# Attention with compressive memory and a gMLP mixer: the order of small work in each attention step, and the end of the attention phase

## The chip, the cores and the metric

The kernel runs on one core of a Trainium2 chip. The metric is the time of one execution on the device in microseconds, as a median over several runs. A core has engines that each run their own list of instructions in order: PE (matrix products, into PSUM), DVE (vector work), ACT (functions and casts), POOL (more vector work), and SP, which here issues nearly all DMA transfers. They wait for one another through semaphores.

## The reference

x has 2048 rows of 640. Two equal layers follow one another; each adds an attention block and then a mixer block to x, and each block begins with a layer norm:

```
x = x + A(layernorm(x));  x = x + B(layernorm(x));  x = x + A(layernorm(x));  x = x + B(layernorm(x))

A: q, k, v = x @ wq, x @ wk, x @ wv          # 32 heads of 20, 4 segments of 512 rows
   for each segment:
       p     = softmax(q k^T / sqrt(20) + mask)   # mask: 0 where the key is at or before the query, else -1e9
       a_dot = p @ v
       a_mem = (phi(q) @ M) / (phi(q) @ z + 1e-6) # phi(t) = t + 1 if t > 0, else exp(t)
       o     = g * a_mem + (1 - g) * a_dot        # g = sigmoid(beta), one per head
       M, z  = M + phi(k)^T @ v, z + sum of phi(k)
   return o @ wo

B: z = gelu(x @ w_in);  z1, z2 = halves of z
   g = w_sp @ layernorm(z2) + b_sp                # w_sp mixes the 2048 rows
   return (z1 * g) @ w_out
```

All is float32. Products are formed from fp16 pairs: each operand is split into a high part and a low part (the cast, and what the cast left), and high times high, high times low and low times high are summed in PSUM.

## The kernel before

Each layer has three stages. **phase1a** is the attention, **phase1b** the layer norm and the first product of the mixer (w_in) with its gelu, **phase2** the mixing over rows and the product with w_out. The change touches phase1a and the seam to phase1b.

*phase1a* (the class Attention) handles 64 pairs of heads, 16 in each of the 4 segments. `run` walks over steps t from -16 to 164, five for every two pairs. Each step writes instructions for different pairs at different distances: `by_queries` forms scores mp whose row maxima mxs are taken on DVE (L1316, L1319); `by_keys` forms scores es transposed, whose exponential P (named Pb for some pairs) is taken on ACT (L1293); `cast` makes P's high part PH on ACT (L1328) and its low part PL (L1332), in two halves of 640 columns, on POOL; `pvs` multiplies PH and PL with the values into one PSUM bank named pv (L1366); `combine` scales that by the row sums and adds it to the memory's part, on DVE (L1377 to L1387, the last addition into gm at L1387). The bank pv has one buffer: pv of a pair starts when combine of the pair before has read its bank out.

Between these stand denser pieces of work, interleaved by their planned times: `unit` makes the queries and keys of 128 channels (five units to a segment, unit (0,0) the first; L1111, tiles qps and kps), with the splits and features of `out` behind them (L1125 to L1156: khl, qhl, relu, phl); `value` the values (vps, L1052); `project` the output product for 12 of the 16 row tiles (yps, L1084); `update` adds a unit's keys and values to the memory (mup, L1209) and copies the result, masked, to mst (L1215); `read` multiplies mst with the query features (num, L1180); `prep` takes the row norms of the next row tiles of x (statistics L305 to L308, the norm at L1033, splits L320 and L321, a DMA transpose L322) into xt. The last pair of a unit also writes out the unit's output halves ohl (casts L1402 and L1403, DMA L1406). num, mup and some small products share a second bank, tagged "ms", with one buffer.

PE's order is the order in which all this is written. What DVE, ACT, POOL and SP do, and in what order, a scheduler sets from the order of writing, from priorities and from named instructions that must be issued first (`issue_after`). Small work that must not stand in front of others is put off with `post(k, f)` to a list `later` of the step k on, and from there it is written before that step's products; a second list, `half`, is written in the middle of the step.

The last pairs have no later work beside them. With TAIL = 1, the low parts of pair 63 are made by POOL for its first head, and for its second head by DVE, written two steps later.

*phase1b* goes over 16 row tiles in the order 0, 8, 1, 9, and so on. For each, `attn_out` takes the rows x1 (loaded at L359; for tiles 12 to 15 it first makes their output product yp, L378), their statistics and norm (for tiles 0 and 8 xn on ACT at L391 and xnhl at L400 and L401), and the split is transposed by DMA into th (L402). Then two products with halves of w_in give zp (L412) for z1 and z2, followed by gelu (L425, L448). In layer 1 the first half of w_in comes as raw chunks wst (L129), split into wi (L81, L82). x1 has two buffers, xn and xnhl one each.

Of the kernel before, what the change touches and what calls it, by code (L numbers as in the profile page):

```python
# [8 lines left out]
F32 = mybir.dt.float32  # L9
# [328 lines left out]
def phase1b(g, o_d, x, x1_d, z1_d, zh, zl):  # L338

    nc, tc = g.nc, g.tc  # L340
    with ExitStack() as ctx:
# [4 lines left out]
        if not g.wsp_scaled:  # L346
            nc.sync.dma_start(g.bsp, g.b_sp.rearrange("(t p) -> p t", p=128))
        g.wi[0].paired(wp0)
        wi0 = g.wi[0].load(g.prep[0], 864, "wr")
# [66 lines left out]
        z2 = {}  # L416
        g.loaded, g.gelu, g.lo = {}, {}, {}

# [31 lines left out]

        with tc.high_priority(offset=3 * HP2):
            a = load(0)
        with tc.high_priority(offset=HP2):
            xn = attn_out(0, *a)
            a = load(ORDER[1])
            th = xn_t(*xn)
        for i, t in enumerate(ORDER):
# [3 lines left out]
            if i + 1 < NT:  # L461
                xn = attn_out(ORDER[i + 1], *a)
            z2_half(t, w_in_half(1, *th))
# [454 lines left out]
class Attention:  # L918
# [9 lines left out]
    def __init__(self, g, x, o_d, x1_d):  # L928
        self.g, self.nc, self.tc = g, g.nc, g.tc
        self.x, self.o_d, self.x1_d = x, o_d, x1_d  # L930
        self.st = g.st
        self.gm = {}
        self.phq = {}
        self.P = {}
        self.pv, self.sum, self.o = {}, {}, {}
        self.mem, self.last, self.stacked, self.waiting = False, -1, -1, False
        self.now, self.later, self.half, self.rd = None, {}, {}, set()
        self.lead = []

    def post(self, k, f, c=None, into=None):  # L940

# [4 lines left out]
        while c is not None and (t % 5 not in c or t in self.rd or t - 1 in self.rd):  # L946
            t += 1
        (self.later if into is None else into).setdefault(t, []).append(f)

# [147 lines left out]
    def unit(self, s, m):  # L1097

        g, nc = self.g, self.nc
        xh, xl = self.xt[s % 2][:, 0], self.xt[s % 2][:, 1]  # L1100
        for nm in "qk" if s else "kq":
            if nm == "k" and self.mem:
# [95 lines left out]
    def update(self, s, m):  # L1198
# [19 lines left out]

        self.post(1, out)

    def stack(self, nm, s, m, hl):
# [5 lines left out]
        nc.sync.dma_start(rows[:, i:i + 2], hl)  # L1227
        if nm == ("k" if s else "q"):
            self.stacked = NU * s + m
# [92 lines left out]
    def cast(self, n, h):  # L1322
# [6 lines left out]

        def low(engine):  # L1330
            for c in (slice(0, 640), slice(640, 1280))[::-1 if n % 2 and h else 1]:
                engine.tensor_tensor(PL[:, c], P[:, h, c], PH[:, c], ALU.subtract)  # L1332

        if h == 0 or n < self.N - self.TAIL:
            low(nc.gpsimd)
        else:
            self.post(2, lambda: low(nc.vector))
        self.P[n, h] = (PH, PL)
# [14 lines left out]
    def pvs(self, n, h, s, m, h0):  # L1353
        nc = self.nc
        PH, PL = self.P.pop((n, h))
        if h == 0:
            pv = self.po.tile([128, 512], F32, tag="pv", name="pv")
            self.pv[n] = pv[:, :8 * 42].rearrange("p (h t c) -> p t h c", h=2, t=4)
            self.sum[n] = pv[:, 8 * 42:8 * 62].rearrange("p (h t c) -> p h t c", h=2, t=4)
# [10 lines left out]
    def combine(self, n, s, m, h0):  # L1370
# [5 lines left out]
        rs = self.pl2.tile([128, 4, 2], F32, tag="rs", name="rs")  # L1376
        nc.vector.tensor_tensor(rs, T[:, :, :, DH], g.iomg[:, h0:h0 + 2].unsqueeze(1).to_broadcast((128, 4, 2)), ALU.mult)  # L1377
        nc.vector.reciprocal(rs, rs)
# [3 lines left out]
        if s > 1:  # L1382
# [3 lines left out]
            nc.vector.tensor_tensor(a, a, wide(DH), ALU.mult)  # L1386
            nc.vector.tensor_tensor(o, a, o, ALU.add)  # L1387
        else:
# [18 lines left out]

        self.post(2, out)

    def run(self, nseg=NSEG):  # L1410
# [82 lines left out]
        def fills():  # L1493

            for t, k, i in sorted(ev):
# [3 lines left out]
                else:  # L1499
                    for d, f in zip((2, 4), self.prep(i)):  # L1500
                        self.post(d, f)

# [57 lines left out]
        for t in range(-LEAD, END):  # L1560
# [33 lines left out]
            with self.behind(DVE):  # L1594
                until(t + 1)
        assert not self.half
        for t in sorted(self.later):
            self.now = None
            for f in self.later[t]:
                f()  # L1600

# [74 lines left out]
```

## Time and profile before

| | |
|---|---|
| median of 3 runs | 2218.08 us (2214.55 to 2218.99) |
| profiled execution | 2217.2 us, its span 2215.5 us |
| mean granted clock of PE | 0.991 |
| PE busy | 2087.8 us, 94% of the span |
| DVE, POOL, ACT busy | 1625.6, 1402.7, 1250.9 us |
| attention of layer 1 | from 0 to about 594 us |
| mixing over rows in layer 1 | 840 to 1115 us |
| attention of layer 2 | from about 1115 to 1677 us |

A row of the timeline has the start, the duration, the engine, the source line, the operation, its result and operands, and in brackets how long the engine stood idle before it and what it waited for. With xN, N neighbouring instructions are one row and the duration is that of all. A row of the waits has the waiting instruction, what released it, the time in all, the number of waits, and the longest. A row of windows has a stretch of time, its length, the busy time of PE, PEld, DVE, ACT and POOL, then PE's granted clock, the DMA share and GB/s.

### The profile page before, as it was taken

The page shows a single profiled execution, that of the slowest core. Times are in us where ns is not written, and L with a number is a line of the kernel's source. Part 1 is how long each engine was busy: PE and PEld are TensorE (multiplying, and loading weights), DVE is VectorE, ACT ScalarE, POOL GpSimd, SP SyncE. Part 2 cuts the span into 40 slices and gives each one's busy share as a digit, 9 for nine tenths or more (in the row PEclk, how much of TensorE's full clock was granted, in tenths as well). Part 3 has the DMA queues.
Part 4 walks back from the last instruction along what each step waited for, and adds up shares of the span by engine and source line. Part 5 has one row for each costly group of instructions (what it writes and reads, how often), then busy time and mean ns, then how long its engine had stood idle before and what let it go on. Part 6 is the DMA issues. An engine that isn't in the chain of part 4 may idle for free.

```text
span 2215.5 us, 53079 instructions
## 1 busy us (share of the span) xinstructions
PE 2087.8 (94%) x21322; PEld 1265.2 (57%) x21322; DVE 1625.6 (73%) x2889; ACT 1250.9 (56%) x1641; POOL 1402.7 (63%) x1172
## 2 busy tenths in 40 slices
PE   5998888999899999999999989989999999999999
PEld 3555655666545555555555556656665555555555
DVE  7788788788587758888657787787875764675563
ACT  4588788788644433333326987878884433333331
POOL 3387898788645345566414889888894433674660
PEclk9999999999999999999999999999999999999999
DMA  6666557344776686666455456553455335876752
GB/s 177 163 174 184 133 163 197 96 121 126 185 199 182 162 278 171 170 183 178 137 167 131 112 139 153 126 118 90 123 141 145 106 110 185 217 175 171 177 142 82
DMA packets 537703, 342.79 MB, mean 155 GB/s; under 512 B 411600, under 2 KB 463312, under 8 KB 537456
## 3 DMA queue, kind: packets, MB, share of 16 engines
q1 hardware_dynamic: 537456, 339.39, 57.2%
q8 instruction: 167, 2.74, 0.5%
q14 instruction: 80, 0.66, 0.1%
HBM read 159.18 MB, written 92.55 MB: 114 GB/s over the span
## 4 chain that ended last, share of the span: by engine, by line
PE 67%; DVE 14%; ACT 7%; issue 4%; DMA 4%; POOL 3%; SPq 1%; ACTq 0%; DVEq 0%; POOLq 0%
PE ga L670 12%; PE zp L412 11%; PE cyp L706 7%; PE pv L1366 4%; PE qps L1111 4%; PE vps L1052 3%; PE gb L670 3%; PE mp L1255 3%; PE yps L1084 3%; DVE mxs L1319 3%; PE gc L670 3%; PE gd L670 3%; PE kps L1111 2%; PE es L1255 2%; ACT PH L1328 2%
## 5 line engine op out<-in xcount | busy, mean ns | idle before, releaser
L1332 POOL TENSOR_TENSOR PL<-P,PH 128x640 f16<-128x640 f32 x384 | 535.1, 1422 | 86.7 <-PE pv L1366 67.9
L1319 DVE TENSOR_REDUCE mxs<-mp 128x2 f32<-128x1024 f32 (+2 forms) x384 | 320.2, 861 | 123.4 <-PE mp L1246 121.3
L1293 ACT ACTIVATE P<-es,sc 128x1024 f32<-128x1024 f32 (+1 forms) x256 | 271.6, 1061 | 102.0 <-PE es L1246 95.8
L640 POOL TENSOR_TENSOR ts<-ts,wt 128x512 f32<-128x512 f32 x196 | 283.3, 1457 | 11.0
L412 PEld LDWEIGHTS <-th 128*128 128x128 f16 x1920 | 188.0, 98 | 169.6 <-issue 6.9
L1328 ACT CAST PH<-P 128x1280 f16<-128x1280 f32 x192 | 239.7, 1249 | 2.5 <-PE pv L1366 1.0
L670 PEld LDWEIGHTS <-wts 128*128 128x128 f16 x1536 | 150.2, 98 | 134.0 <-issue 5.5
L670 PE MATMUL ga<-zh,wts 128*128 128x432 f16 x768 | 210.8, 346 | 4.5 <-ACT u L737 4.5
L308 POOL TENSOR_TENSOR lnrs<-lnve,mhalf 128x1 f32<-128x1 f32 x96 | 59.8, 631 | 230.2 <-DVE lnve L307 223.1
L1332 POOL TENSOR_TENSOR PL<-Pb,PH 128x640 f16<-128x640 f32 x124 | 175.8, 1447 | 20.3 <-PE pv L1366 19.3
L412 PE MATMUL zp<-wi,th 128*128 128x432 f16 x960 | 181.2, 346 | 3.5 <-ACT z L448 3.5
L640 POOL TENSOR_TENSOR ts<-wt,wt 128x512 f32<-128x512 f16 x28 | 33.9, 1211 | 226.3 <-DMA wt<-wn 226.3
L1052 PE MATMUL vps<-wvh,xt 128*128 128x320 f16 x640 | 154.8, 309 | 23.7 <-DVE relu L1143 13.0
L670 PEld LDWEIGHTS <-wt 128*128 128x128 f16 x1152 | 112.7, 98 | 96.5
L1366 PE MATMUL pv<-vs,PH 128*128 128x41 f16 x2560 | 158.6, 182 | 8.6 <-DVE gm L1387 5.5
L706 PE MATMUL cyp<-wuh,ut 128*128 128x320 f16 (+1 forms) x896 | 163.6, 299 | 2.7 <-DMA ut<-un 1.8
L706 PEld LDWEIGHTS <-ut 128*128 128x128 f16 (+1 forms) x1344 | 131.1, 98 | 57.5 <-DMA ut<-un 4.0
L1255 PEld LDWEIGHTS <-qk 64*128 64x128 f16 (+1 forms) x2048 | 77.9, 94 | 150.1 <-issue 129.3
L1366 PE MATMUL pv<-vs,PL 128*128 128x41 f16 x2560 | 156.3, 181 | 2.6 <-POOL PL L1332 2.6
L412 PE MATMUL zp<-wi1h,th 128*128 128x432 f16 x640 | 149.9, 349 | 2.2 <-DMA th<-xnhl 2.1
L524 DVE SCALAR_TENSOR_TENSOR wn<-wr,wsc,wn 128x512 f16<-128x512 f32 x126 | 92.9, 775 | 76.8 <-ACT wn L523 76.7
L1366 PEld LDWEIGHTS <-PH 128*128 128x128 f16 x2560 | 138.6, 96 | 15.2 <-ACT xnhl L400 2.9
(224 smaller groups left out, 5286.5 us busy)
## 6 DMA issues: line engine op xcount, KB each, us to landing
qk<-st SPq DMA_DIRECT2D x256, 120.0 KB
wr<-in_B_w_sp_dram SPq DMA_DIRECT2D x60, 512.0 KB
z<-z SPq DMA_DIRECT2D x32, 432.0 KB
cz<-z SPq DMA_DIRECT2D x32, 432.0 KB
xt<-in_A_x_dram SPq DMA_DIRECT2D x32, 320.0 KB
st<-khl SPq DMA_DIRECT2D x40, 256.0 KB
st<-qhl SPq DMA_DIRECT2D x40, 256.0 KB
x<-x SPq DMA_DIRECT2D x32, 320.0 KB
```

Source lines behind the costliest of these rows:

```text
L412: nc.tensor.matmul(zp[:, n, :FHH], a[:, k, :], b[:, k, c:c + FHH], start=(k == 0 and j == 0), stop=(k == KD - 1 and j == 2))
L640: nc.gpsimd.tensor_tensor(t, a, t if b == "t" else get(b), ALU.add if op == "+" else ALU.subtract)
L670: nc.tensor.matmul(ps, w[:, a, k % 4, :], z[:, k, j, :], start=start and k == 0 and i == 0, stop=k == NP - 1 and i == 2, skip_group_check= ...
L706: nc.tensor.matmul(yp[:, n, :320], a[:kn[k], k, :], b[:kn[k], k, n * 320:(n + 1) * 320], start=(k == 0 and j == 0), stop=(k == KO - 1 and ...
L1052: nc.tensor.matmul(ps, a[:, k, c], b[:, k, n * 320:(n + 1) * 320], start=(i == 0), stop=(i == 14))
L1111: nc.tensor.matmul(ps, a[:, k, c], b[:, k, :], start=(i == 0), stop=(i == 14))
L1255: nc.tensor.matmul(out[:, h, o:o + w], a[r, ac], b[r, bc], start=o == 0, stop=False, skip_group_check=True)
L1293: g.exp = nc.scalar.activation(P, E, AF.Exp, scale=g.esc)
L1319: e = nc.vector.tensor_reduce(mx[:, :, n, j], mp[:, :, o:o + w], AX.X, ALU.max)
L1328: nc.scalar.copy(PH, P[:, h])
L1332: engine.tensor_tensor(PL[:, c], P[:, h, c], PH[:, c], ALU.subtract)
L1366: nc.tensor.matmul(pv[:, i, h, :41], x[:, c:c + 128], v[:, j, h0 + h, :], start=(j == 0 and x is PH), stop=(j == i and x is PL), skip_grou ...
```

## The change

Five edits, all of order or place; what is computed stays the same.

1. phase1b issues the loads of its first two row tiles (0 and 8) first of all, at a high priority, ahead of the chunks of w_in. Tile 0's norm is issued after the last addition of combine(60) (`g.near[-4]`), tile 8's after that of combine(61).
2. A third list, `end`, is written last in each step. `prep`'s row norms and the output halves of `combine` go there. `update`'s memory copy goes first into its step's list (`first=True`).
3. Unit (0,0) makes its queries first, then its keys, as all units of later segments do.
4. The low parts of pair 63 are made for both heads at once, the first half by POOL, the second by DVE.
5. pv of pairs 61 and 63 takes the bank "ms" instead of the bank pv. The first instruction of combine(62) is issued after the last low part.

```diff
+        g.loaded, g.gelu, g.lo = {}, {}, {}
+        two = [pe2.tile([128, D], F32, tag="x1", name="x1") for _ in range(2)]
+        with tc.high_priority(offset=HP):
+            for t, x1 in zip(ORDER, two):
+                g.loaded[t] = nc.sync.dma_start(x1, x1_d[t])
         g.wi[0].paired(wp0)
...
-        with tc.high_priority(offset=3 * HP2):
-            a = load(0)
         with tc.high_priority(offset=HP2):
-            xn = attn_out(0, *a)
-            a = load(ORDER[1])
+            with tc.issue_after(g.near[-4].ins):
+                xn = attn_out(0, two[0])
+            a = two[1:]
             th = xn_t(*xn)
...
             if i + 1 < NT:
-                xn = attn_out(ORDER[i + 1], *a)
+                with ExitStack() if i else tc.issue_after(g.near[-3].ins):
+                    xn = attn_out(ORDER[i + 1], *a)
...
-    def post(self, k, f, c=None, into=None):
+    def post(self, k, f, c=None, into=None, first=False):
...
-        (self.later if into is None else into).setdefault(t, []).append(f)
+        todo = (self.later if into is None else into).setdefault(t, [])
+        todo.insert(0 if first else len(todo), f)
...
-        for nm in "qk" if s else "kq":
+        for nm in "qk" if s or m == 0 else "kq":
...
-        self.post(1, out)
+        self.post(1, out, first=True)
...
-        def low(engine):
-            for c in (slice(0, 640), slice(640, 1280))[::-1 if n % 2 and h else 1]:
-                engine.tensor_tensor(PL[:, c], P[:, h, c], PH[:, c], ALU.subtract)
-
-        if h == 0 or n < self.N - self.TAIL:
-            low(nc.gpsimd)
-        else:
-            self.post(2, lambda: low(nc.vector))
+        for i, c in enumerate((slice(0, 640), slice(640, 1280))[::-1 if n % 2 and h else 1]):
+            self.low = (nc.vector if i and n >= self.N - self.TAIL else nc.gpsimd).tensor_tensor(PL[:, c], P[:, h, c], PH[:, c], ALU.subtract)
...
-            pv = self.po.tile([128, 512], F32, tag="pv", name="pv")
+            p, tag = (self.pm, "ms") if n in (self.N - 3, self.N - 1) else (self.po, "pv")
+            pv = p.tile([128, 512], F32, tag=tag, name="pv")
...
-        nc.vector.tensor_tensor(rs, T[:, :, :, DH], g.iomg[:, h0:h0 + 2].unsqueeze(1).to_broadcast((128, 4, 2)), ALU.mult)
+        with self.tc.issue_after(self.low.ins) if n == self.N - 2 else ExitStack():
+            nc.vector.tensor_tensor(rs, T[:, :, :, DH], g.iomg[:, h0:h0 + 2].unsqueeze(1).to_broadcast((128, 4, 2)), ALU.mult)
...
-            nc.vector.tensor_tensor(o, a, o, ALU.add)
+            g.near[n - self.N] = nc.vector.tensor_tensor(o, a, o, ALU.add)
...
-        self.post(2, out)
+        self.post(2, out, into=self.end)
...
-                        self.post(d, f)
+                        self.post(d, f, into=self.end)
...
+            with self.behind(DVE):
+                for f in self.end.pop(t, ()):
+                    f()
```

*First place: DVE in the middle of layer 1, at a memory copy (near 382 us of the profile before).* mxs are row maxima, lnst the statistics of a row tile xt, phl a feature's low part, vs the values' low part, mst the memory copy. Before, and then with the change:

```order
L1316 TENSOR_REDUCE mxs_304<-mp 128x2x2
L305 BN_STATS lnst<-xt 128x6 x2
L1153 SCALAR_TENSOR_TENSOR phl<-relu,sc,phl 128x512
L1058 SCALAR_TENSOR_TENSOR vs_298<-vps,vs_298 128x16x20
L1215 TENSOR_TENSOR mst_306<-mup,bmask 128x168
L306 BN_AGGR lnmv<-lnst 128x2
L307 TENSOR_SCALAR lnve<-lnmv 128x1
```

```order
L1322 TENSOR_REDUCE mxs_304<-mp 128x2x2
L1221 TENSOR_TENSOR mst_306<-mup,bmask 128x168
L1159 SCALAR_TENSOR_TENSOR phl<-relu,sc,phl 128x512
L1064 SCALAR_TENSOR_TENSOR vs_298<-vps,vs_298 128x16x20
L305 BN_STATS lnst<-xt 128x6 x2
L306 BN_AGGR lnmv<-lnst 128x2
L307 TENSOR_SCALAR lnve<-lnmv 128x1
```

The copy has moved up past two statistics, phl and vs, to stand right behind the reduction; the statistics have moved down behind phl and vs.

*Second place: SP near the end of the pairs of layer 1.* qk is an operand of the scores, x_0_8 the rows of tile 8, wst a raw chunk of w_in, o_3 the output halves in DRAM. Before, and then with the change:

```order
L1351 DMA qk_293<-mr 2x4x128 x2
L129 DMA wst<-in_B_w_in_dram 128x864 x4
L1076 DMA xt<-in_A_x_dram 128x640
L359 DMA x_11495<-x_0_8 128x640
L1406 DMA o_3<-ohl 128x4x120
```

```order
L352 DMA x_11463<-x_0_8 128x640
L1351 DMA qk_293<-mr 2x4x128
L129 DMA wst<-in_B_w_in_dram 128x864 x4
L1082 DMA xt<-in_A_x_dram 128x640
L1408 DMA o_3<-ohl 128x4x120
```

Tile 8's load has moved from behind the four chunks and one other load to ahead of them.

*Third place: ACT at the last casts of layer 1.* x_11495 before and x_11463 with the change are tile 8, x_11462 is tile 0. Before, and then with the change:

```order
L1328 CAST PH<-P 128x1280
L391 ACTIVATE xn<-x_11495,neg 128x640
L1293 ACTIVATE Pb<-es,sc 128x2x512
L1328 CAST PH<-P 128x1280
L1293 ACTIVATE Pb<-es,sc 128x2x512
L1328 CAST PH<-Pb 128x1280 x2
L400 ACTIVATE xnhl<-xn,lnrs 128x640
```

```order
L1334 CAST PH<-P 128x1280
L396 ACTIVATE xn<-x_11462,neg 128x640
L1299 ACTIVATE Pb<-es,sc 128x2x512
L1334 CAST PH<-P 128x1280
L405 ACTIVATE xnhl<-xn,lnrs 128x640
L1299 ACTIVATE Pb<-es,sc 128x2x512
L1334 CAST PH<-Pb 128x1280 x2
L396 ACTIVATE xn<-x_11463,neg 128x640
```

Tile 8's xn has moved behind the last cast; tile 0's xn and xnhl, which were issued some fifty instructions earlier, stand between the casts.

More of the change, by code (lines that the diff above doesn't have):

```diff
@@ L416, in phase1b @@
         z2 = {}
-        g.loaded, g.gelu, g.lo = {}, {}, {}
         def block(k, j, src):
@@ L936, in __init__ @@
         self.mem, self.last, self.stacked, self.waiting = False, -1, -1, False
-        self.now, self.later, self.half, self.rd = None, {}, {}, set()
+        self.now, self.later, self.half, self.end, self.rd = None, {}, {}, {}, set()
         self.lead = []
-    def post(self, k, f, c=None, into=None):
+        g.near = {}
+    def post(self, k, f, c=None, into=None, first=False):
         if self.now is None:
@@ L1227, in stack @@
         nc.sync.dma_start(rows[:, i:i + 2], hl)
-        if nm == ("k" if s else "q"):
+        if nm == ("k" if s or m == 0 else "q"):
             self.stacked = NU * s + m
@@ L1595, in run @@
                 until(t + 1)
+            with self.behind(DVE):
+                for f in self.end.pop(t, ()):
+                    f()
         assert not self.half
[L1597 to L1600, printed above, removed]
+        self.now = None
+        for left in (self.later, self.end):
+            for t in sorted(left):
+                for f in left[t]:
+                    f()
 def phase1a(g, x, o_d, x1_d, nseg=NSEG):
```

## The prediction

> **What bounds the kernel now.** I read the page first, then the waits of PE over the whole span, then the stretches around the largest of them.
>
> ```profile
> PE 2087.8 (94%) x21322; PEld 1265.2 (57%) x21322; DVE 1625.6 (73%) x2889; ACT 1250.9 (56%) x1641; POOL 1402.7 (63%) x1172
> ...
> PE num L1180 <- DVE lnmv L306: 8.3, 4, 2.7
> PE num L1180 <- DVE mst L1215: 5.6, 8, 1.2
> PE vps L1052 <- DVE relu L1143: 13.0, 7, 4.9
> PE mp L1255 <- DVE mxs L1319: 14.0, 24, 1.3
> PE vps L1052 <- DMA xt<-xnhl: 2.6, 1, 2.6
> PE zp L412 <- DMA th<-xnhl: 2.1, 3, 1.3
> ```
>
> PE is busy 2087.8 of 2215.5 us of span, so no edit that leaves its 21322 matmuls alone can win more than 128 us, plus what a throttled clock costs. The waits (engine, line, what it waited for; us in all, times, longest) say which part of this the edits can touch. They remove no arithmetic: they are reorderings, and each is worth the share of such a wait that it takes away.
>
> ```profile
> 45.00:50.00 5.00, 3.09 (x7) 0.85 (x8) 5.00 (x11) 3.66 (x5) 0.00 (x0) 0.56 0.22 64
> 230.00:235.00 5.00, 3.95 (x40) 2.38 (x40) 2.99 (x5) 2.70 (x4) 2.22 (x2) 0.50 0.85 198
> 385.00:390.00 5.00, 5.00 (x48) 4.08 (x48) 1.73 (x3) 1.13 (x2) 0.25 (x1) 0.50 0.17 33
> ```
>
> In these 5 us windows (PE's busy time first, the granted clock the third number from the end) a second cost is seen: around the long waits PE's clock is down to 0.50 or little more, so a wait costs its length and then up to half of the next 5 us.
>
> **Part 1, queries first in unit (0,0).** PE, ACT and DVE at the start of layer 1:
>
> ```profile
> 45.84 1.03 PE L1111 MATMUL kps<-xt,wkh 128*128 128x512 f16 x2 [3.14 <-ACT wkh L81]
> 52.96 0.59 PE L1111 MATMUL qps<-xt,wqh 128*128 128x512 f16 x2
> 44.95 3.70 ACT L81 ACTIVATE wkh<-wstl,iv 128x640 f16<-128x640 f32 x5
> 44.90 1.66 DVE L82 SCALAR_TENSOR_TENSOR wql<-wsth,iv,wqh 128x640 f16<-128x640 f32 x2
> 48.72 2.47 DVE L82 SCALAR_TENSOR_TENSOR wkl<-wstl,iv,wkh 128x640 f16<-128x640 f32 x3
> ```
>
> The weights of the queries are split first and the keys are multiplied first. PE has nothing from 42.7 (45.84 less 3.14) to 45.84, then runs the 15 matmuls of kps at 3.09/7 = 0.44 us each under a clock of 0.56, and those of qps from 52.96, 0.65 per three (0.59 for two, and the third), to 56.2. With queries first, qps can start at 42.7 and is bound by the last wql, ready at 44.90 + 1.66 = 46.56: done about 46.9. kps then follows its splits, whose last part ends at 48.72 + 2.47 = 51.19, and ends about 51.8. That is 56.2 - 51.8 = 4.4. Were all 15 kps cold, 46.9 + 15 x 0.44 = 53.5, a gain of 2.7. I take **4.0**, bounds 2.5 to 4.5. In layer 2 the weights are there already, and I take nothing.
>
> **Part 2, memory copies first and row norms last in each step.** The copy mst (L1215) releases num on PE. At the costliest kind of place (the first of the places shown with the change), DVE issues it right behind the reduction mxs now, no longer behind two statistics, phl and vs.
>
> ```profile
> 381.70 0.88 DVE L305 BATCH_NORM_STATS2 lnst<-xt 128x6 f32<-128x320 f32 x2
> 383.55 0.32 DVE L1215 TENSOR_TENSOR mst<-mup,bmask 128x168 f32<-128x168 f32 x1
> 384.01 0.55 PE L1180 MATMUL num<-mst,phq 128*128 128x126 f32 x1 [2.65 <-DVE lnmv L306]
> ```
>
> The wait is put down to lnmv, but it is mst that num reads. Issued at 381.70 instead of 383.55, mst is done near 382.0 and num starts 1.85 earlier; the rest of the 2.65 is the reduction, which stays ahead. The four waits of this kind (8.3) give 8.3 x 1.85/2.65 = 5.8. The eight waits on mst itself (5.6, 0.7 each) mostly have one 0.6 to 0.7 instruction taken from in front of the copy, and I count two thirds, 3.7. The exponential of the keys that vps waits for at 231 stands behind a row norm and an output half on ACT:
>
> ```profile
> 226.88 0.72 ACT L320 CAST xnhl<-xt 128x640 f16<-128x640 f32 x1 [0.89 <-DVE xt L1033]
> 229.00 0.71 ACT L1402 CAST ohl<-gm 128x640 f16<-128x640 f32 x1
> 229.61 0.66 ACT L1138 ACTIVATE kps<-kps,sc 128x512 f32<-128x512 f32 x1
> 231.05 0.43 PE L1052 MATMUL vps<-wvh,xt 128*128 128x320 f16 x1 [4.90 <-DVE relu L1143]
> ```
>
> Both casts now stand behind it: 0.72 + 0.71, and part of the 0.89 in which ACT waited for the norm, together 1.9 of 4.90. The order at the other waits on relu is as it was. So 5.8 + 3.7 + 1.9 = 11.4. After 384 the clock was 0.50 over all of 385 to 390; with the wait down to 0.8 that stretch should be warm, 5 x 0.5 = 2.5 more, and the one after 231 I leave cold.
>
> The Trainium skill, "TensorE: Matmul & The Clock Gate", section "What's actually happening", has the clock fall to half after an idle window of some 3.4 us and come back after a busy one of that length. By it the wait at 231, cut from 4.90 to 3.0, would keep the clock up there too, an estimated 2.5 more; the rows speak against trusting that, since 2.65 before 384 was enough.
>
> Nothing is removed: statistics (0.88, and some 0.3 behind them), xt and casts come later in the step, and something is behind them. PE waited for mxs in 24 places, 14.0 in all, and moved work of about 1.2 can lengthen any wait of that kind. Twelve row tiles in each of two layers are normed beside the pairs: at worst 24 x 1.2 = 29, at best 0. With DVE busy 73% of the span, and most reductions never waited for (24 waits), I take a seventh, 4. Part 2 is 11.4 + 2.5 - 4, about **10**, bounds 2 to 16.
>
> **Part 3, the end of the pairs in layer 1.** What happened there, from SP's queue through DVE, POOL and ACT to PE:
>
> ```profile
> 570.65 0.43 SPq L359 DMA_DIRECT2D x<-x  x1
> 579.02 0.89 DVE L305 BATCH_NORM_STATS2 lnst<-x 128x6 f32<-128x320 f32 x2 [4.74 <-DMA x<-x]
> 580.74 0.55 POOL L308 TENSOR_TENSOR lnrs<-lnve,mhalf 128x1 f32<-128x1 f32 x1 [2.89 <-DVE neg L390]
> 583.63 1.11 ACT L1293 ACTIVATE Pb<-es,sc 128x1024 f32<-128x1024 f32 x1
> 584.83 2.42 ACT L1328 CAST PH<-Pb 128x1280 f16<-128x1280 f32 x2
> 580.75 0.83 ACT L391 ACTIVATE xn<-x,neg 128x640 f32<-128x640 f32 x1 [3.89 <-DVE neg L390]
> 581.25 5.48 POOL L1332 TENSOR_TENSOR PL<-P,PH 128x640 f16<-128x640 f32 x4
> 586.69 3.35 POOL L1332 TENSOR_TENSOR PL<-Pb,PH 128x640 f16<-128x640 f32 x2
> 587.95 2.77 DVE L1332 TENSOR_TENSOR PL<-Pb,PH 128x640 f16<-128x640 f32 x2
> 592.24 0.20 PE L1366 MATMUL pv<-vs,PH 128*128 128x41 f16 x1 [2.56 <-DVE gm L1387]
> 593.63 0.89 PE L412 MATMUL zp<-wi1h,th 128*128 128x432 f16 x2
> 584.12 2.09 SPq L402 DMA_TRANSPOSE th<-xnhl  x1
> 590.93 0.83 ACT L400 ACTIVATE xnhl<-xn,lnrs 128x640 f16<-128x640 f32 x1 [3.68 <-DMA th<-xnhl]
> ```
>
> Tile 8's load stands behind four wst loads and lands 8.3 us after its issue; its statistics hold DVE 4.74, and through them POOL's lnrs 2.89 and ACT's xn 3.89. Pair 62's low parts are behind lnrs, and its casts behind xn. Tile 8 is now fetched ahead of the four (second place shown with the change), and on ACT its norm has changed places with the last casts (third place). Tile 0's norm, done some 50 us earlier until now, has come into the tail; tile 8's has left it. Without the waits POOL goes on when it became free, at 580.74 - 2.89 = 577.85: lnrs 0.55, pair 62 5.48, tile 8's lnrs 0.55, and of pair 63 one half of each head, 2 x 1.4: 587.2. The second halves run beside on DVE, and pv(63), now with a bank of its own, need not wait for combine(62)'s gm (the 2.56): it ends near 588, against the 593.63 at which zp, the product behind it, began. But the first matmul behind it reads tile 0's th. That transpose follows on SP the load of tile 9, which needs tile 8's buffer, hence tile 8's xn, now ACT's last. ACT from 576.87 (580.75 - 3.89): xn 0.83, Pb 1.11, one PH 1.21, xnhl 0.83, Pb 1.11, two PH 2.42, xn 0.83, about 585. Issued at 585.5, the transpose took 6.8 before (584.12 to 590.93, beside other transfers) and in layer 2 at most 3.2 (below): it lands between 588.7 and 592.3. I take 589.6, so **4.0** is won, bounds 1 to 5.5.
>
> The split itself has a price. A low part takes 5.48/4 = 1.37 on POOL alone, 3.35/2 = 1.68 beside DVE, and on DVE 0.8 to 2.0:
>
> ```profile
> L1332 DVE TENSOR_TENSOR PL<-Pb,PH x4: 812/1278/2014, 587.9 to 1673.6; 128x640 f16<-128x640 f32 x4
> ```
>
> The Trainium skill, "SBUF — State Buffer", section "Who interferes with whom", makes a DVE instruction with two inputs from SBUF and a GpSimd one that reads SBUF shut each other out for a whole instruction. By it two halves on each engine take 2 x 1.37 + 2 x 0.81 = 4.4 instead of 2.8, and pv(63) would end at an estimated 589.6 and not 588. The four of before ran from 586.69 to 590.72, 4.03, so the trace mostly agrees; th covers it in my sum.
>
> **Part 4, the same in layer 2.** No wst loads there, so less is late.
>
> ```profile
> 1668.18 1.35 SPq L402 DMA_TRANSPOSE th<-xnhl  x1
> 1671.38 0.83 ACT L400 ACTIVATE xnhl<-xn,lnrs 128x640 f16<-128x640 f32 x1
> 1675.53 0.18 PE L1366 MATMUL pv<-vs,PH 128*128 128x41 f16 x1 [2.26 <-DVE gm L1387]
> ```
>
> pv(63) ended at 1675.53 + 1.4 (as from 592.24 to 593.63), about 1677. The bank takes the 2.26 away. But ACT has tile 0's xn and xnhl in front of its last casts (+1.66, against tile 8's xn, 0.83, gone from there), so xn(8) ends about 1671.6, and tile 0's transpose is issued near 1672.2 and not 1668.18; 3.2 later (1668.18 to 1671.38, when its source was free again) it is 1675.4, with 6.8 it would be 1679. I take **1.5** won, bounds -2 to 3.
>
> **Part 5, the mixer's first products.** The group of zp's matmuls on the page:
>
> ```profile
> L412 PE MATMUL zp<-wi,th 128*128 128x432 f16 x960 | 181.2, 346 | 3.5 <-ACT z L448 3.5
> ```
>
> In layer 1, PE's order behind the pairs changes (all 30 of tile 0's second product before tile 8), tile 8's transpose stands behind a wst load and two wust loads. 60 matmuls now cover it, at 0.346 us 21 us. I take **0**, bounds -3 to 3: all waits of this product on th are 2.1.
>
> **Sum.** 4.0 + 10 + 4.0 + 1.5 + 0 = 19.5 against the profiled execution's 2217.2: 2197.7. The median shown is 0.9 above that execution; I predict **2198**.
>
> **Rivals.** *The middle gives nothing* (the norms postponed are waited for one step on): parts 1, 3, 4 alone, 9.5, 2208. For it: 73% on DVE as a mean, more beside the pairs. Against: num is the waiter in 12 places and the copy passes only work that nobody on PE waited for. *The clock stays up as well* at 231 and in the head: 2.5 after 231 and another 2.5 each in the twin places of layer 2 and the head, and no give-back (4): 19.5 + 11.5, 2186. *Slower: late rows.* A row tile normed at the end of the step is transposed later, and vps waits for its xt. Each costs up to 1.2; from 17 of the 24 on, all 19.5 is gone, and with all 24 it is 29 - 19.5, 2227. For it: that wait exists (2.6). Against: it exists once. *The change does little*: the scheduler leaves the waits, and only the bank at 592 counts, 2 to 3: 2215.
>
> **Chances.** Forecast 0.62, middle nothing 0.19, clock 0.09, slower 0.06, little 0.04. A difference under 0.2% (4.4 us) can't be told from no change here. Faster: 0.62 + 0.09 + 0.16 of the 0.19 = 0.87; same 0.07; slower 0.06. The range of 8 in 10 is 2184 to 2212: the bounds of part 2 alone give 8 up and 6 down, the tails and the mixer 6 more, taken as not all one way.
>
> **What would show it.** Waits of num down from 13.9 to about 4; the kps wait of 3.14 gone and the first unit done near 52; in the tail no DVE wait of 4.74 and zp starting 4 us earlier behind pv(63); the clock of the window behind 384 at 1. I am wrong if waits on mxs rise by more than 8, if vps waits on xt, or if zp waits for th at either tail longer than 3 us.

## The result and the profile after

The changed kernel takes 2195.33 us in the median (2190.82 to 2199.39, 5 runs), against 2218.08 (2214.55 to 2219.97, 5 runs). The ratio is 0.9895, with a 95% interval of 0.9879 to 0.9911: faster by 22.75 us in the medians, 1.05% by the ratio. The prediction was 2198, in a range of 2184 to 2212. The profiled execution has a span of 2193.7 us against 2215.5.

The page of the kernel after, and its waits of PE (what waited, for what; us in all, times, longest):

```profile
PE 2080.7 (95%) x21322; PEld 1260.2 (57%) x21322; DVE 1627.6 (74%) x2889; ACT 1250.4 (57%) x1641; POOL 1404.1 (64%) x1172
...
PE mp L1261 <- DVE mxs L1325: 15.9, 24, 1.4
PE vps L1058 <- DVE relu L1149: 11.9, 8, 2.9
PE zp L417 <- DMA th<-xnhl: 8.1, 7, 1.8
PE pv L1367 <- POOL PL L1337: 6.6, 7, 1.4
PE num L1186 <- DVE mst L1221: 5.5, 8, 0.8
PE vps L1058 <- DMA xt<-xnhl: 3.0, 1, 3.0
```

The waits of num, 13.9 before on two rows, are one row of 5.5: four of the twelve are gone and none is longer than 0.8. The waits of pv on gm and of kps on wkh are no longer there. Other rows have grown: zp on th from 2.1 to 8.1, pv on POOL's low parts PL from 2.6 to 6.6, and mxs from 14.0 to 15.9. PE's work is the same 21322 matmuls, and its busy time fell by 7.1 us (2087.8 to 2080.7), with a mean granted clock of 0.996 instead of 0.991; in the other 14.7 of the 21.8 us of span PE no longer stands idle.

The same matmul can be found in both traces, so the gain can be read along the program. The table gives by how much the profile of the change got ahead of the profile of before (minus) or lost (plus) in each stretch.

| stretch | us |
|---|---|
| start to the first score product mp of layer 1 | -5.6 |
| to pv of pair 60 | -4.2 |
| to the end of the last pv | -2.9 |
| from there to the first zp of the mixer | +1.2 |
| to the first matmul of the row mixing | -0.4 |
| row mixing, to the first pv of layer 2 | +1.2 |
| to pv of pair 60 | -9.9 |
| to the end of the last pv | -0.9 |
| from there to the first zp | +2.0 |
| to the first matmul of the row mixing | -1.4 |
| to the end | -1.1 |

These sum to -22.0 after rounding; the last matmul stands at -22.2, the end of the span at -21.8. A stretch of one execution is uncertain by one to three us: kernels that differ from before in nothing in a stretch still differ there by that much (in the row mixing of layer 1, by +0.4 to +3.6 over all profiles of this document).

At the first memory copy that the prediction priced, on DVE and PE, and the clock (third number from the end) of the windows behind it, ahead of it and behind the wait for relu:

```profile
376.41 1.23 DVE L1322 TENSOR_REDUCE mxs<-mp 128x4 f32<-128x1024 f32 x1 [3.62 <-PE mp L1252]
377.56 0.32 DVE L1221 TENSOR_TENSOR mst<-mup,bmask 128x168 f32<-128x168 f32 x1
378.02 0.46 PE L1186 MATMUL num<-mst,phq 128*128 128x126 f32 x2 [0.81 <-DVE mst L1221]
...
380.00:385.00 5.00, 5.00 (x95) 3.64 (x92) 4.55 (x9) 3.53 (x4) 3.90 (x4) 1.00 0.70 51
370.00:375.00 5.00, 3.36 (x17) 2.28 (x17) 1.99 (x6) 3.67 (x5) 5.00 (x5) 0.66 0.80 208
225.00:230.00 5.00, 5.00 (x44) 2.98 (x43) 3.15 (x6) 2.85 (x3) 4.96 (x4) 0.50 1.02 231
```

The wait of 2.65 is 0.81 and the clock behind it 1.00 where it was 0.50. Part of the slow clock has only moved: from 370 to 375 us it is 0.66, where before it was 1.00. The wait for relu, 4.90 before, is 2.88 here (at 224.48), and the clock behind it is still 0.50.

The end of the pairs in layer 1, on SP, ACT, POOL, DVE and PE:

```profile
557.89 0.32 SPq L352 DMA_DIRECT2D x<-x  x1
577.46 0.32 SPq L364 DMA_DIRECT2D x<-x  x1
577.87 1.33 SPq L407 DMA_TRANSPOSE th<-xnhl  x1
569.54 0.83 ACT L396 ACTIVATE xn<-x,neg 128x640 f32<-128x640 f32 x1 [2.50 <-DVE neg L395]
576.61 0.82 ACT L396 ACTIVATE xn<-x,neg 128x640 f32<-128x640 f32 x1
569.52 0.55 POOL L308 TENSOR_TENSOR lnrs<-lnve,mhalf 128x1 f32<-128x1 f32 x1 [1.51 <-DVE neg L395]
570.04 6.06 POOL L1337 TENSOR_TENSOR PL<-P,PH 128x640 f16<-128x640 f32 x4
576.07 1.13 POOL L308 TENSOR_TENSOR lnrs<-lnve,mhalf 128x1 f32<-128x1 f32 x1
577.17 3.34 POOL L1337 TENSOR_TENSOR PL<-Pb,PH 128x640 f16<-128x640 f32 x2
568.83 0.55 DVE L1096 SCALAR_TENSOR_TENSOR xt<-yps,sc,xt 128x320 f32<-128x320 f32 x1 [3.35 <-PE pv L1367]
569.36 0.14 DVE L395 TENSOR_SCALAR neg<-lnmv 128x1 f32<-128x1 f32 x1
573.28 1.57 DVE L406 SCALAR_TENSOR_TENSOR xnhl<-xn,lnrs,xnhl 128x640 f16<-128x640 f32 x1 [1.01 <-ACT xnhl L405]
575.63 1.16 DVE L1337 TENSOR_TENSOR PL<-Pb,PH 128x640 f16<-128x640 f32 x1 [0.66 <-issue]
577.53 1.72 DVE L1337 TENSOR_TENSOR PL<-Pb,PH 128x640 f16<-128x640 f32 x1
580.56 0.19 PE L1367 MATMUL pv<-vs,PL 128*128 128x41 f16 x1 [0.77 <-POOL PL L1337]
582.03 0.54 PE L417 MATMUL zp<-wi1h,th 128*128 128x432 f16 x2 [1.01 <-DMA th<-xnhl]
```

Tile 0's split is done on DVE at 574.85. But tile 8's xn ends on ACT at 577.43, tile 9's load is issued at 577.46, and only then tile 0's transpose at 577.87; zp starts when that has landed. DVE no longer waits 4.74 for a load. In layer 2 the first zp waits 1.83 for th at 1656.90.

### The profile page after: what moved, and what is told of

It is laid out like the page before. It is cut to its first block, busy times and chain, and to the rows that moved or that the text cites. A ratio compares the mean times of both kernels' runs of the same rounds, so it can differ in the third digit from the quotient of the medians.

```text
span 2193.7 us, 53096 instructions
## 1 busy us (share of the span) xinstructions
PE 2080.7 (95%) x21322; PEld 1260.2 (57%) x21322; DVE 1627.6 (74%) x2889; ACT 1250.4 (57%) x1641; POOL 1404.1 (64%) x1172
## 4 chain that ended last, share of the span: by engine, by line
PE 71%; DVE 11%; ACT 6%; DMA 5%; issue 3%; POOL 3%; SPq 1%; ACTq 0%; DVEq 0%; POOLq 0%
PE zp L417 14%; PE ga L674 12%; PE cyp L710 7%; PE pv L1367 4%; PE qps L1117 4%; PE vps L1058 4%; PE yps L1090 3%; PE mp L1261 3%; PE gb L674 3%; PE gc L674 3%; PE gd L674 3%; DVE mxs L1325 2%; PE kps L1117 2%; PE es L1261 2%; POOL PL L1337 2%
## 5 line engine op out<-in xcount | busy, mean ns | idle before, releaser
L417 PEld LDWEIGHTS <-th 128*128 128x128 f16 x1920 | 187.6, 98 | 172.0 <-DMA th<-xnhl 10.9
L1261 PE MATMUL mp<-qk 60*128 60x512 f16 (+3 forms) x1024 | 126.0, 303 | 21.2 <-DVE mxs L1325 15.9
```

Source lines behind the costliest of these rows:

```text
L417: nc.tensor.matmul(zp[:, n, :FHH], a[:, k, :], b[:, k, c:c + FHH], start=(k == 0 and j == 0), stop=(k == KD - 1 and j == 2))
L1261: nc.tensor.matmul(out[:, h, o:o + w], a[r, ac], b[r, bc], start=o == 0, stop=False, skip_group_check=True)
```

## The experiments

Kernels with the same median for before ran beside the same runs of it, on one chip. The ratio is that to the kernel before. The whole change itself (0.9895) ran beside other runs of before, so it is compared with these kernels by the ratios.

| kernel | median us | before | ratio (95% interval) |
|---|---|---|---|
| before with queries first alone | 2213.53 | 2219.89 | 0.9972 (0.9960 to 0.9984) |
| before with the second edit alone | 2202.76 | 2219.89 | 0.9922 (0.9901 to 0.9942) |
| before with the edits at the end alone | 2216.73 | 2219.89 | 0.9985 (0.9974 to 0.9996) |
| the change, tile 0's transpose earlier | 2192.44 | 2219.89 | 0.9876 (0.9856 to 0.9895) |
| before with the copy first alone | 2203.25 | 2218.20 | 0.9934 (0.9911 to 0.9957) |
| before with norms and halves last alone | 2211.73 | 2218.20 | 0.9963 (0.9946 to 0.9980) |
| the change without the two banks | 2195.83 | 2218.20 | 0.9897 (0.9880 to 0.9914) |
| the change, transpose earlier, tile 0's norm early | 2191.60 | 2218.20 | 0.9876 (0.9858 to 0.9895) |
| the change, norms and halves not last | 2194.89 | 2219.87 | 0.9887 (0.9855 to 0.9919) |
| the change, loads not first | 2191.37 | 2219.87 | 0.9867 (0.9849 to 0.9885) |
| the change, low parts as before | 2198.07 | 2219.87 | 0.9894 (0.9870 to 0.9918) |
| as the eighth, tile 8's norm later | 2198.75 | 2219.87 | 0.9898 (0.9879 to 0.9917) |

### Queries first alone

```diff
-        for nm in "qk" if s else "kq":
+        for nm in "qk" if s or m == 0 else "kq":
```

> The kernel before with queries first in unit (0,0) and nothing else. Where the profile of the whole change stood 5.6 us ahead of before at the first score product, it stood only 2.8 ahead at the product pv of pair 8. Theory A (the early queries themselves run into later waits: a wait of 1.3 on a qk row transfer near 80 us and one of 2.4 on qhl near 130 us): this kernel is 5.6 ahead at the first score product and about 2.8 ahead from pair 8 on, about 2215. Theory B (the row norms put off cost that 2.8): it stays 5.6 ahead through the phase, about 2212.5.

Measured: 0.28% faster, 6.2 us by that ratio, and the first score product is 3.7 ahead in its profile. It keeps 3.8 at pv of pair 8, and the row transfer and qhl waits that theory A blamed are not there. So theory A falls. Theory B falls too: in the run with the earlier transpose, which has the row norms put off as well, pv of pair 8 stands 5.2 ahead, and 4.2 to 5.7 in the five others below that have both. The dip to 2.8 in the profile of the whole change belonged to that execution. The profile of this kernel ends level with that of before: it loses 1.5 in the mixer's first products and 3.0 in the row mixing of layer 1, and 2.1 in layer 2 between pairs 8 and 60, where its code is the same; the timed runs decide on the total, and the profile only on where things stand early on.

### The second edit alone, and its halves

The first of the three runs has both parts, the second only the memory copy (the first line below), the third only the output halves and the row norms (the other two):

```diff
-        self.post(1, out)
+        self.post(1, out, first=True)
...
-        self.post(2, out)
+        self.post(2, out, into=self.end)
...
-                        self.post(d, f)
+                        self.post(d, f, into=self.end)
```

> The kernel before with only the second edit: memory copies first, row norms and output halves last in each step. If the parts add up, it gains what the whole change gained between the first pairs and pair 60: about 4 in layer 1 and 9 to 10 in layer 2, together 12 to 14, about 2205. Rival: the parts do not add, because waits only move on to the next release; then 6 or less, 2212 or more. Under theory B of the run on the queries it also loses 2 to 3 between pairs 4 and 8 of layer 1.

> The kernel before with only the memory copy first in its step's list; row norms and output halves stay where they were. The second edit as a whole gave 17 in the median and, in its profile, took the waits of num from 13.9 to 5.5. Theory (the copy's place is what counts): the waits of num on lnmv, 8.3 in 4, go here already, with the slow clock behind two of them: 8 to 11 in all, 2209 to 2211; the wait of vps near 231 (4.9) stays. Rival (the norms' place is what counts, the copy was only behind them): 0 to 3, 2216 or more.

> The kernel before with only row norms and output halves last in each step; the copy stays behind what was written before it. Theory: the wait of vps near 231 falls from 4.9 to 2.9, the copy has lost the two statistics in front of it but still stands behind phl and vs (1.2), so that the waits of 2.65 before num fall by about 0.9 each; 4 to 7 in all, 2212 to 2215. If both this and the copy alone come near 17, each alone does the work of the other; if they sum to much less than 17, they need each other.

Measured: 17.1, 15.0 and 6.5 us in the medians. The first two are above what was expected (12 to 14 and 8 to 11), the third within (4 to 7). From the first score product of layer 1 to pair 60, and from the first pv of layer 2 to pair 60, the three profiles together win 17.9, 17.0 and 7.0. The waits of num, of the copy alone and then of the norms alone:

```profile
PE num L1181 <- DVE mst L1216: 5.5, 8, 0.8
PE vps L1053 <- DVE relu L1144: 10.4, 7, 2.9
```

```profile
PE num L1180 <- DVE mst L1215: 12.1, 12, 3.1
PE vps L1052 <- DVE relu L1143: 10.7, 8, 2.5
```

The copy alone takes num to 5.5, all that the whole change reaches. The norms alone leave all twelve waits. Three of the four long ones fall by 0.8, near the 0.9 expected: 1.51 and 1.52 to 0.73, and the 2.65 of layer 2 to 1.86. The 2.65 of layer 1 rises to 3.09. DVE and POOL there, and then at the same place of layer 2, norms alone:

```profile
377.57 1.23 DVE L1316 TENSOR_REDUCE mxs<-mp 128x4 f32<-128x1024 f32 x1 [2.07 <-PE mp L1246]
378.71 1.96 DVE L1153 SCALAR_TENSOR_TENSOR phl<-relu,sc,phl 128x512 f16<-128x512 f32 x1
381.00 0.32 DVE L1215 TENSOR_TENSOR mst<-mup,bmask 128x168 f32<-128x168 f32 x1
374.66 5.47 POOL L1332 TENSOR_TENSOR PL<-P,PH 128x640 f16<-128x640 f32 x4
```

```profile
1463.43 1.23 DVE L1316 TENSOR_REDUCE mxs<-mp 128x4 f32<-128x1024 f32 x1 [2.07 <-PE mp L1246]
1464.57 0.74 DVE L1153 SCALAR_TENSOR_TENSOR phl<-relu,sc,phl 128x512 f16<-128x512 f32 x1
1465.63 0.32 DVE L1215 TENSOR_TENSOR mst<-mup,bmask 128x168 f32<-128x168 f32 x1
1460.64 5.93 POOL L1332 TENSOR_TENSOR PL<-P,PH 128x640 f16<-128x640 f32 x4
```

With the statistics gone from in front of it, phl follows the reduction 0.8 sooner, but in layer 1 it takes 1.96 and not 0.7: it starts while POOL is at its low parts and ends 0.54 after POOL does (374.66 + 5.47 = 380.13, 378.71 + 1.96 = 380.67). The copy behind it is not earlier for it: it starts 3.43 after the reduction did, and 2.99 in the kernel before. In layer 2 phl also begins beside POOL's low parts and takes 0.74, while POOL's four take 5.93 instead of 5.47; there the copy starts 2.20 after the reduction did. So DVE was held up at one place, and POOL at the other. The Trainium skill, "SBUF — State Buffer", section "Who interferes with whom", has a DVE instruction with two inputs in SBUF contend with a GpSimd instruction that reads SBUF, and issue order decide which of the two blocks; the two places agree with it. Moving the statistics, 0.88, is then no gain where phl is the one that is held up.

So the first theory holds for num: the copy's place is what counts. It does not hold for the wait near 231. The copy alone shortens it to 2.9 as well, as its rows on ACT and DVE show:

```profile
221.87 0.32 DVE L1216 TENSOR_TENSOR mst<-mup,bmask 128x168 f32<-128x168 f32 x1
222.11 0.68 DVE L1130 SCALAR_TENSOR_TENSOR khl<-kps,khl 128x512 f16<-128x512 f32 x1
222.71 0.82 DVE L1034 TENSOR_SCALAR xt<-xt,lnmv,lnrs 128x640 f32<-128x640 f32 x1
223.79 0.65 ACT L1139 ACTIVATE kps<-kps,sc 128x512 f32<-128x512 f32 x1
224.35 0.72 ACT L320 CAST xnhl<-xt 128x640 f16<-128x640 f32 x1
```

Written first, the copy and khl also come ahead of the row norm xt in the scheduler's order, and the norm's cast xnhl falls behind the exponential kps. Either half of the edit brings this about, so the two share that gain: alone they give 15.0 and 6.5, together 17.1.

### The whole change without norms and halves last

```diff
-        self.post(2, out, into=self.end)
+        self.post(2, out)
...
-                        self.post(d, f, into=self.end)
+                        self.post(d, f)
```

> The whole change with row norms and output halves put back where they were before; the copy stays first. The copy alone gave 15 of the 17 that both gave, and the norms alone 6. Theory (once the copy is first, the norms' place is worth 1 to 3): 2196.5 to 2198. Rival (the norms' place and the copy overlap wholly): 2195, no difference from the whole change. Other rival (beside the edits at the head and the end the norms matter more, as the sum of the parts alone, 26, is more than the whole's 23): 2199 or more.

Measured: 2194.89, ratio 0.9887 against 0.9895 of the whole change, the intervals lying one in the other. The waits of num are 5.5 and of mxs 15.9 + 2.2, as in the whole change. Once the copy is first, the third list adds nothing that these runs can tell: the second expectation (no difference) is the nearest, but the two intervals together leave some 8 us either way.

### The edits at the end alone

The whole change with the edits to the queries, the copy and the third list taken out.

> The kernel before with the edits at the end of the pairs alone: early loads, low parts on two engines, two banks. Theory: the last product pv ends 3 earlier in layer 1 and 1 earlier in layer 2, but the first mixer product waits for the transposed rows of tile 0, so only 1 to 2 in layer 1 is kept and layer 2 loses about 1 at that point; with what the mixer's first products give back, 0 to 3 in all, 2215 to 2218. Rival: without the early start of the other edits the tile-0 rows are in time and the whole 4 or 5 is kept, 2213.

Measured: 0.15% faster (3.3 us by the ratio, 0.9 to 5.8 by its interval). From pv of pair 60 to the last pv 3.0 and 0.9 are won in the two layers, and to the first zp 1.7 and 0.6 are kept. The first theory holds in layer 1, zp waits 1.16 for th there; in layer 2 it does not lose what the theory said. A profile alone would not show this gain: four kernels that lack the edits at the end (the queries, the second edit, and its two halves) also stand 0.1 to 1.5 ahead of before from pair 60 to the first zp of layer 1.

### Tile 0's transpose ahead of tile 9's load

```diff
             if i + 2 < NT:
-                a = load(ORDER[i + 2])
+                with ExitStack() if i != 1 else tc.issue_after(th0.ins):
+                    a = load(ORDER[i + 2])
```

Here th0 is the transpose of tile 0.

> The whole change, and the transpose of tile 0's rows put ahead of the load of tile 9 on SP's queue. Theory (that load waits for tile 8's buffer, which ACT frees after its last cast, and holds the transpose up): the transpose is issued 3 us earlier in layer 1 and 2.3 earlier in layer 2, the waits of 1.0 and 1.8 of the first mixer product go, 2 to 3 us less than the whole change, 2192 to 2193. Rival: the transpose is slow because of other transfers or the norm itself, and the waits stay, 2195.

SP, and PE's first product behind the pairs, layer 1:

```profile
574.90 1.34 SPq L407 DMA_TRANSPOSE th<-xnhl  x1
580.58 0.20 PE L1369 MATMUL pv<-vs,PL 128*128 128x41 f16 x1 [0.77 <-POOL PL L1339]
580.87 0.35 SPq L364 DMA_DIRECT2D x<-x  x1
```

Measured: 2192.44. The transpose is issued 2.97 earlier (574.90, where the pairs before run 1.35 ahead of the whole change's), and both first zp follow the last pv without a wait for th. That the queue held the transpose back is shown. What was won differs: in layer 2 zp stands 2.0 better than in the whole change, measured from pair 60; in layer 1 0.2 worse, since there pv itself came 1.4 later, behind a wait of 2.45 for an exponential that stood 1.07 in the whole change. The medians differ by 2.9; the intervals overlap.

### The change without the two banks, with the low parts as before, and with the loads not first

```diff
-            p, tag = (self.pm, "ms") if n in (self.N - 3, self.N - 1) else (self.po, "pv")
+            p, tag = self.po, "pv"
```

> The whole change with pv of pairs 61 and 63 back in the bank of the others. Theory: pv of pair 63 waits again for combine of pair 62, which is issued after the last low part (ends near 581.0 in the profile of the whole change), so pv ends 2 later; since the first mixer product waited for tile 0's rows anyway (1.0 and 1.8), only about 1 and 0.5 show at that point: 2196 to 2197.5. Rival, as the sum had it: the bank alone carried the 2.56 and 2.26 of the two waits, 2200.

```diff
-        for i, c in enumerate((slice(0, 640), slice(640, 1280))[::-1 if n % 2 and h else 1]):
-            self.low = (nc.vector if i and n >= self.N - self.TAIL else nc.gpsimd).tensor_tensor(...)
...
+        if h == 0 or n < self.N - self.TAIL:
+            low(nc.gpsimd)
+        else:
+            self.post(2, lambda: low(nc.vector))
```

> The whole change with the low parts of pair 63 as before: the first head's by POOL, the second head's by DVE, written two steps later. Theory: two halves on each engine in either case, but the second head's start later; pv of pair 63 ends 0.5 to 1.5 later, and behind the wait for tile 0's rows (1.0 and 1.8) nothing of it shows: 2195 to 2196.5. Rival: the split is needed for what the end gained, 2198.

```diff
-        with tc.high_priority(offset=HP):
-            for t, x1 in zip(ORDER, two):
-                g.loaded[t] = nc.sync.dma_start(x1, x1_d[t])
...
+        for k, (t, x1) in enumerate(zip(ORDER, two)):
+            with tc.high_priority(offset=(1 if k else 3) * HP2):
+                g.loaded[t] = nc.sync.dma_start(x1, x1_d[t])
```

> The whole change with the two loads of tiles 0 and 8 at their former priority, so that tile 8's load stands behind the four chunks of w_in on SP again. Theory: in layer 1 tile 8's statistics wait on DVE as before (4 to 5), with the last pairs' combine and low parts behind them, and the first mixer product of layer 1 starts 4 to 6 later than with the whole change; layer 2, without these chunks, 0 to 1: 2199 to 2202. Rival: the tile-0 rows set the end anyway, 2195 to 2197.

Measured: 2195.83, 2198.07 and 2191.37, ratios 0.9897, 0.9894 and 0.9867. From pair 60 to the first zp of layer 1 the three win 1.5, 1.4 and 2.1, the whole change 1.8. In layer 2 they stand at 0.0, -0.4 and +1.0, the whole change at +1.1.

Without the banks the wait for gm is back, 2.06 before pv at 579.06, and from pair 60 the last pv of layer 1 ends 1.4 later than in the whole change, but the first zp is only 0.2 later, because in the whole change it waits 1.0 for th, and here it follows pv without a wait. The theory holds and its small remainder is not seen. The low parts' order is worth nothing that shows at the first zp (0.3 worse in layer 1, 1.5 better in layer 2), as the first theory had it; that run's median is 2.7 above the whole change, at the 2198 of the rival, but its ratio is the same. The last of the three contradicts what I expected: the early load does nothing for the end. Its rows on SP and DVE:

```profile
558.57 0.44 SPq L454 DMA_DIRECT2D x<-x  x1
567.96 0.32 DVE L1389 TENSOR_TENSOR gm<-pv,gm 128x160 f32<-128x160 f32 x1
568.20 0.88 DVE L305 BATCH_NORM_STATS2 lnst<-x 128x6 f32<-128x320 f32 x2
579.57 0.54 PE L414 MATMUL zp<-wi1h,th 128*128 128x432 f16 x2 [1.17 <-DVE pv L1388]
```

Tile 8's load is again issued behind the four chunks (558.57), but its statistics stand behind the last addition of combine(61), and at 568.20, 9.6 after the issue, DVE does not wait for them. So moving the statistics is enough to take the 4.74 away, and the early load is not needed for it; whether the early load alone would do it was not run. Loading first costs if anything: this run is the fastest in the median, though its interval overlaps that of the whole change.

### Tile 0's norm early, then tile 8's later

```diff
-            with tc.issue_after(g.near[-4].ins):
-                xn = attn_out(0, two[0])
+            xn = attn_out(0, two[0])
```

on top of the earlier transpose; the second run has in addition `near[-2]` for `near[-3]`.

> The whole change with the transpose of tile 0's rows ahead of tile 9's load, and with the norm of tile 0 where it was before (not put off to the end of the pairs). Theory: the tail loses 1.66 on ACT, a statistics pass, 1.6 of a low half on DVE and one power on POOL; the waits of pv on POOL (1.4 and 0.8) shrink, and pv of the last pair ends 1 to 2 earlier in each layer than with the transpose alone: 2189 to 2191. Rival: POOL's own low parts set the end (5.5 a pair) and nothing changes, 2192.5; or the norm disturbs the steps before, 2194 or more.

> The whole change with tile 0's transpose ahead of tile 9's load, tile 0's norm at its former place, and tile 8's norm only after combine of pair 62 instead of 61. In the same without the last point, one power of tile 8's norm stands on POOL in front of the last pair's low parts, and the first product after the pairs starts 5 earlier in both layers than with the whole change. Theory: POOL's low parts start 0.55 to 1.1 sooner, pv of pair 63 ends that much sooner, and tile 8's rows, two products later, are still in time in layer 1 and late by about 1 in layer 2: 2190 to 2191.5. Rival: tile 8's rows are late in both layers, by 2 to 4 each: 2194 to 2198.

Measured: 2191.60 and 2198.75. With the norm early, POOL runs eight low halves without a break (560.59 to 571.51), and from pair 60 to the first zp 5.0 and 1.9 are won in the two layers, against 1.8 won and 1.1 lost in the whole change. Nothing of that shows in the ratio, which is the same as with the earlier transpose alone (0.9876). Its profile gave back 3.4 us in layer 2 before pair 8 against that kernel, where all engines run the same instructions in the same order, so this belongs to the execution; why the timed runs show no gain stays open. Tile 8's rows, two products later, are already waited for: 1.49 and 1.77 (1.07 and 2.32 with the earlier transpose alone). With tile 8's norm later as well, 5.1 and 2.5 are won, and then tile 8's rows are late:

```profile
590.68 0.90 PE L417 MATMUL zp<-wi1h,th 128*128 128x432 f16 x2 [2.94 <-DMA th<-xnhl]
1670.44 0.54 PE L417 MATMUL zp<-wi1h,th 128*128 128x432 f16 x2 [2.05 <-DMA th<-xnhl]
```

From the first zp to the row mixing of layer 1 this kernel loses 5.8 on before; the waits for th in between are 10.9 in all, and 6.1 with the norm early alone. The rival holds, and a little more than it said (2198.75 against 2194 to 2198): the rows of tile 8 had nothing to spare.

## Why the prediction was right, and where it was not

**The total** was 2 to 3 us off (2198 against 2195.33), and that close by luck in part, because errors in the parts cancelled: in the profile of the change parts 1 and 2 gave 5.7 more than forecast, parts 3 and 4 4.8 less.

**Part 1**, 4.0 with bounds 2.5 to 4.5: the mechanism was right, and so was the size. kps no longer waits for wkh, and the clock there, 0.56 before, is 1.00. The windows of 30 to 35 and 45 to 50 us of the profile of the change:

```profile
30.00:35.00 5.00, 2.89 (x22) 2.11 (x23) 4.03 (x10) 0.45 (x1) 0.00 (x0) 1.00 0.96 245
45.00:50.00 5.00, 4.57 (x17) 1.06 (x15) 5.00 (x13) 2.92 (x5) 0.00 (x0) 1.00 0.11 37
```

From the end of the value products ahead of it the first unit took 13.7 before (42.7 to 56.4) and takes 9.1 now (41.3 to 50.4): 4.6 less, where the working had 4.4. That the first score product stands 5.6 ahead has a second cause, which is luck: PE came to the unit 1.4 earlier. Before, the clock from 30 to 35 us was 0.70, and here it is 1.00. Of the nine profiles with the new start, six have such slow clock ahead of the unit, as before has, and stand 3.4 to 4.3 ahead; three do not, and stand 4.8 to 5.7 ahead. The timed runs of this edit alone give 6.2, with an interval of 3.6 to 8.9.

**Part 2**, 10 with bounds 2 to 16: 4.2 and 9.9 in the two stretches of the profile of the change, 14.1, and 17.1 in the median alone (13 to 22 by its interval), above the upper bound. The term for num was nearly right, 9.5 predicted (4.4 to be left) and 8.4 found, but its halves were off in opposite ways: the waits put down to lnmv gave 6.7 of 8.3 (5.8 predicted), those on mst 1.8 of 5.6 (3.7 predicted). The 1.9 near 231 were priced rightly; they were put down to the casts' place alone, and the copy's place brings them too. Two terms were mis-sized. The give-back of 4: waits on mxs rose by 1.9 and 0.4 (15.9 from 14.0, 3.0 from 2.6), and the one wait of vps for xt is 3.0 against 2.6. And the clock, counted at 2.5: on the same matmuls, PE's busy time in the two stretches is 4.2 less in the profile of the change and 5.8 less in that of the second edit alone.

The estimate by the Trainium skill ("TensorE: Matmul & The Clock Gate", section "What's actually happening") that the clock would stay up behind 231 did not come true: a wait of 2.88 is followed by 0.50. But the prediction's reason against it, that 2.65 was enough before 384, does not hold by itself. In layer 2 of the kernel before the same wait is followed by a clock of 1.00:

```profile
1475.00:1480.00 5.00, 5.00 (x96) 3.70 (x96) 4.01 (x8) 3.14 (x3) 2.97 (x3) 1.00 0.04 8
```

**Part 3**, 4.0 with bounds 1 to 5.5: 1.8. That the first product would wait for tile 0's transpose behind tile 9's load was right, and the run that moved the transpose shows it. Two sizes were wrong. POOL does not go on when it became free: tile 0's own statistics hold it, since their last part (neg at 569.36) stands on DVE behind the sum of an output product (568.83, which waited 3.35); lnrs waited 1.51, ACT's xn 2.50. And POOL's work is longer where DVE has its two-input work beside it (573.28 to 579.25): 6.06 for 5.48, 1.13 for 0.55, 3.34 for 2.8, 1.7 in all. The last pv ended 2.9 ahead where 5.6 were expected. And the first cause that I named, the load behind four chunks, was not what the end needed, as the run with the loads late shows.

**Part 4**, 1.5 with bounds -2 to 3: lost 1.1 at the first zp, through the wait of 1.83 for th, on the side that the working named; 1.4 came back in the products behind it, where the clock before had been low after its wait (0.72 from 1675 to 1680, 1.00 with the change). The working also passed over a wait: before, DVE stood 3.54 for tile 8's load in layer 2 as well, where no chunk of w_in is ahead of it.

```profile
1658.15 0.89 DVE L305 BATCH_NORM_STATS2 lnst<-x 128x6 f32<-128x320 f32 x2 [3.54 <-DMA x<-x]
```

With the change that wait is gone too, and the last pv ended 0.9 ahead. **Part 5**, 0: 0.4 won in layer 1.

**The rivals.** The likeliest case came. That the middle gives nothing is out. "The clock stays up as well" did not come true at 231, nor at its twin in layer 2, where a wait of 2.84 is followed by 0.66 from 1310 to 1315; in the head the clock did stay up, but part 1 had that in its sum. Late row tiles of x did not come up: the wait for xt is still one, of 3.0.

**What stays open** is how the head's and the end's gains add. The three groups alone give 6.4, 17.1 and 3.2, 26.7, and the whole change 22.75. The intervals of the four together allow either that they add or that some 4 are lost; no run tells.

## What to carry to other kernels

Ask of a late instruction which result the waiting engine reads, and move that one result's producer up, rather than its neighbours down: here one copy moved past a few instructions gave 15 us alone, of the 23 of the whole change, and a whole list of work put off, 6.5 alone, gave nothing more beside it that the runs can tell. An in-order queue passes a wait on to all behind it, so for each transfer that matters look at what the ones ahead of it wait for: a load for a later tile, waiting for its buffer, held the one transpose that was needed for 3.0 us (574.85 to 577.87). And undo each part on its own, since the cause that the profile suggests (a load that landed late) can be cured by another part of the same change.

## What was not expected of the hardware

A DVE instruction with two inputs in SBUF took 1.96 instead of 0.74 us where it began beside POOL's low parts and ended 0.54 after them, and so a DVE instruction that is started earlier need not end earlier; at the same place of the other layer it took 0.74, and POOL's work was longer by 0.46. Half clock followed a wait of PE of 2.88 us, and did not follow one of 0.81; a wait of 2.65 had it behind it in one layer and not in the other. And the same code, in the same order on every engine, differed between executions by up to 3.4 us in a stretch of 60 us, so a single profile can't tell a gain of that size.
